# Seven block products in another order across two PSUM banks, with a re-ordered operand split and a new table of rank offsets

## The chip, the cores and the metric

One NeuronCore of one Trainium2 chip. The metric is the device time of one execution in microseconds (us), as a median of several runs. A profile is one further execution of the same program, with its own time.

## The reference

Attention on q, k, v of shape 8 x 8 x 576 x 64 (batch, head, position, channel): a softmax attention over positions averaged in fours, repeated back to 576 positions, plus a softmax attention in a band of 7 positions. The sum is laid out as 4608 rows of 512 and goes through a two-layer block:

```python
    x = np.ascontiguousarray(attn_out.transpose(0, 2, 1, 3)).reshape(B * S, H * D)   # 4608 x 512
    h = x @ w_in                        # 512 x 2048
    g = np.maximum(0.01 * h, h)
    return (g @ w_out).astype(np.float32)   # 2048 x 512
```

Nearly all of TensorE's work is the two matrix products.

## The kernel before

Every fp32 matrix product is made of three fp32r matmuls (high x high, high x low, low x high parts), so each operand exists as a high and a low half. The 4608 rows are cut into twelve chunks of 256 to 512 columns. The first nine chunks use a plain product (line 1120) for the first layer. The last three chunks have 512 columns each, and their first layer is worked out with seven block products in place of eight (a Strassen-Winograd scheme) for each pair of blocks of the 2048 features: eight groups for a chunk, 24 groups in all, which I number G0 to G23. This runs from about 640 us to the end.

A group is the function `products`. It has two PSUM banks. Bank b1 holds the halves y and v, bank b2 the halves z and x; a half is 128 x 256. A block product is six matmuls of 256 columns into one half (line 1149). In the order in which TensorE's queue has them before the change, with the scheme's numbers:

- product 1 into x (b2), product 2 into y (b1), product 5 into v (b1), product 7 into z (b2), product 6 into x (b2, on top of 1), product 3 into v (b1, on top of 5), product 4 into z (b2, on top of 7).

Beside them, with `mix` as one SBUF tile of three thirds: ScalarE (ACT) copies product 1 out of x and later the sum "u2" out of x (both line 1158), and product 5 out of v (1158). VectorE (DVE) makes the joint sum p57 of products 5 and 7 (line 1179: one of them read from its bank, the other from `mix`). At the end DVE adds two thirds of `mix` to each whole bank (line 1164), `leaky` applies the activation with two ACT instructions (1210, 1211) and a DVE subtraction (1213), and the result is gh, gl, of which there are three buffers each.

The second layer (`down_proj`, line 1245) takes gh and gl. Its unit is three matmuls of 512 columns into one of four accumulators; a group yields eight such units, which I call "downs". They have no tie to a place between the products: a planner (class `Order`) puts all work into one order ahead of time, by modelled start times, ranks, and the offsets of the table `SHIFTS` (task number: offset of its rank). The queue of each engine is then fixed, and an instruction on the chip waits by semaphores for what it needs, as tracked for whole tiles.

Weights of products 5, 6, 7 and 3 are sums of blocks that come from DRAM in each group: `feed` loads r0 (blocks of products 5 and 6) and then r1 (blocks of products 7 and 3), 512 KB each, from the POOL queue (line 588). There is one buffer of each, so r0 is asked for after product 6 of the group before, and r1 after its product 3.

`operands` makes the seven right-hand operands T0 to T6 of a chunk (`split`: an ACT copy and a subtraction, lines 471 and 474; `less`: a DVE subtraction into PSUM, line 481). T0 to T6 belong to products 1, 2, 5, 6, 7, 3, 4 in this order.

Of the kernel before, what the change touches and what calls it, by code (L numbers as in the profile page):

```python
# [13 lines left out]
ALU = mybir.AluOpType  # L14
# [29 lines left out]
HN = 256  # L44
# [27 lines left out]
def pieces(j0, j1):  # L72
# [13 lines left out]
RATE = 270e3  # L86
SAFE = 0.4
SHIFTS = {
# [16 lines left out]
}  # L105
POLICIES = [SHIFTS]
SCARCE, HURRY = ("pt",), 1000
# [139 lines left out]
def attn_moe(policy, ctx, tc, qkt, vd, vs3, qkb, vb, vwb, band, identb, w_in, w_out, ident, out, sums):  # L247
    nc = tc.nc
# [8 lines left out]
    od = Order(bufs, policy)  # L257

    def slot(*tags):
        return (yield ("slot", tags, 0))  # L260
# [16 lines left out]
    def op(eng, n, *after, times=1, port=False):  # L277
        if eng == "PE":
            dur = n
        else:  # L280
            a, k = COST[eng]
            dur = times * a + k * n
        return (yield ("op", eng, dur, max((0.0,) + after), 0, port or eng == "POOL"))
# [9 lines left out]
    def wait(name, n=1):  # L293
        return (yield ("wait", name, n))
# [144 lines left out]
    def bank_of(s):  # L439
        return (s // 3 + FIRST + 1) % 2  # L440
# [15 lines left out]
    def operands(i):  # L456
        tx = yield from wait(("x", i), LANDED[i])
        (b11, t1), (b21, b22) = ([x[:, :, :HN], x[:, :, HN:]] for x in xt[i])

        def taken(s):  # L460
            if i == FIRST:
                t = yield from wait(("up", LAST[-1])) if s == 6 else wait(("emptied", bank_of(s)))
            h = yield from slot(f"t{s}")
            if i == FIRST:
                h.t = t
            return h

        def split(s, h, x, t, own=True):
            hi, lo = put(i, s)
            t = yield from op("ACT", 2 * HN, t, h.t)  # L470
            nc.scalar.copy(out=hi, in_=x)
            eng = pick("DVE", "POOL") if own else "DVE"
            t = yield from op(eng, 2 * HN, t, port=own)
            (nc.vector if eng == "DVE" else nc.gpsimd).tensor_tensor(out=lo, in0=x, in1=hi.bitcast(F32), op=ALU.subtract)  # L474
            od.signal(("T", i, s), t)
            ready[i, s] = h
            return t

        def less(out, x, y, *after, port=False):
            t = yield from op("DVE", 2 * HN, *after, port=port)  # L480
            nc.vector.tensor_tensor(out=out, in0=x, in1=y, op=ALU.subtract)
            return t

        h = yield from taken(0)
        yield from split(0, h, b11, tx)
        h = yield from taken(1)
        yield from split(1, h, b21, tx)
        h = yield from taken(2)
        yield from split(2, h, t1, tx)
        s_2, s_3 = yield from two("pt")  # L490
        t2 = bank(s_2).rearrange("p (c m) -> p c m", c=2)
        t = yield from less(t2, b22, t1, tx, s_2.t, port=True)
        t3 = bank(s_3).rearrange("p (c m) -> p c m", c=2)
        tt = yield from less(t3, t2, b11, t, s_3.t)
        h = yield from taken(3)
        t = yield from split(3, h, t2, t, False)
        t = yield from less(t2, b21, t2, t, tt)
        h = yield from taken(4)
        s_3.free((yield from split(4, h, t3, tt, False)))
        h = yield from taken(5)  # L500
        tb = yield from split(5, h, b22, tx)
        h = yield from taken(6)
        t = yield from split(6, h, t2, t, False)
        s_2.free(t)
        return max(t, tb)
# [86 lines left out]
    def pick(*engines):  # L592
        return min(engines, key=lambda e: od.engine[e] + (0.5 if e == "POOL" else 0.0))
# [534 lines left out]
    def products(i, ch, j):  # L1128
# [4 lines left out]
        mix = sb(s_m, [128, 3 * HN], F32)  # L1133
# [3 lines left out]
        def product(out, ws, s, first, *after):  # L1137
            to = yield from wait(("T", ch, s))
            held = None
            if isinstance(ws, int):  # L1140
                after += ((yield from wait(("fed", ch, j, ws // 2))),)
                held = fed.pop((ch, j, ws // 2)) if ws % 2 else None
                x = odd[ws // 2][0]
                ws = tuple([x[:, ws % 2, k, c * 128:c * 128 + 128] for c in range(2)] for k in range(2))
            t = yield from op("PE", 0.702, to, *after)
            (wh, wl), (xh, xl) = ws, put(ch, s)
            for c in range(2):
                for k, (a, b) in enumerate(((wh, xh), (wh, xl), (wl, xh))):
                    nc.tensor.matmul(out, a[c], b[:, c], start=first and c + k == 0, stop=c == 1 and k == 2, skip_group_check=True)  # L1149
            if held:  # L1150
                held.free(t)
            if last:
                ready[ch, s].free(t)
            return t

        def copied(name, out, src, t):
            t = yield from op("ACT", HN, t, s_m.t)
            nc.scalar.copy(out=out, in_=src)  # L1158
            od.signal((name, i), t)
# [7 lines left out]
        a11, a12, a22 = block(2 * j, 0), block(2 * j, 1), block(2 * j + 1, 1)  # L1167
        tw = max((yield from wait(("w", 2 * j, 0))), (yield from wait(("w", 2 * j + 1, 0))))
        t = yield from product(x, a11, 0, True, tw, s_2.t)
        od.spawn(-10, copied("p1", mix[:, :HN], x, t))  # L1170
        yield from product(y, a12, 1, True, s_1.t)
        t = yield from product(v, 0, 2, False)
        od.spawn(-10, copied("p5", mix[:, 2 * HN:], v, t))
        t = yield from product(z, 2, 4, False)

        def joint(t):
            t5 = yield from wait(("p5", i))
            t = yield from op("DVE", HN, t, t5)
            nc.vector.tensor_tensor(out=mix[:, 2 * HN:], in0=z, in1=mix[:, 2 * HN:], op=ALU.add)  # L1179
            od.signal(("p57", i), t)  # L1180

        od.spawn(-10, joint(t))
        tc1 = yield from wait(("p1", i))
        t = yield from product(x, 1, 3, False, tc1)
        od.spawn(-10, copied("u2", mix[:, HN:2 * HN], x, t))
        tc5 = yield from wait(("p5", i))
        t1 = yield from product(v, 3, 5, False, tc5)

        def first(t):
            t = yield from added("b1", b1, 0, t, (yield from wait(("u2", i))))  # L1190
# [1 line left out]
            od.spawn(-10, leaky(i, 2 * HN, s_1, b1, t))  # L1192

        od.spawn(-10, first(t1))
        tm = yield from wait(("p57", i))
        t2 = yield from product(z, a22, 6, False, tm)

        def second(t):
            t = yield from added("b2", b2, 1, t, (yield from wait(("u2", i))))
# [219 lines left out]
```

## Time and profile before

| | |
|---|---|
| median of 3 runs | 928.11 us (927.41 to 929.78) |
| the profiled execution | 926.15 us |
| its span, first to last instruction | 924.4 us |
| TensorE (PE) matmuls busy | 896.7 us, 97% |
| PE weight loads (PEld) busy | 841.2 us, 91% |
| DVE, ACT, POOL busy | 657.8, 459.8, 616.4 us |

PE works on its matmuls in a pipeline, so a gap reads best on PEld, the weight load ahead of each matmul: there is one for each matmul, and its row says how long it sat idle and what ended that.

### The profile page before, as it was taken

What the parts mean: (1) busy time and instruction counts of PE and PEld (TensorE: products, weight loads), DVE (VectorE), ACT (ScalarE), POOL (GpSimd) and SP (SyncE); (2) the same over time, 40 slices, a digit from 0 to 9 for tenths busy, and PEclk for the clock granted to TensorE, in tenths of its full rate; (3) what the DMA queues carried; (4) which work ended last, traced back from release to release, by engine and by line L of the source; (5) the groups of instructions that cost most, each with busy time, mean ns of one, the idle gap of its engine ahead of it and who ended that gap; (6) DMA issues with size and microseconds to landing.
All of it is one profiled execution on the core that took longest, in us unless ns stands there. A gap on an engine that the chain in (4) does not pass through costs nothing.

```text
span 924.4 us, 17453 instructions
## 1 busy us (share of the span) xinstructions
PE 896.7 (97%) x6400; PEld 841.2 (91%) x6400; DVE 657.8 (71%) x1134; ACT 459.8 (50%) x1426; POOL 616.4 (67%) x354
## 2 busy tenths in 40 slices
PE   5899999999999999999999999999999999998998
PEld 4699999999999999999999999999888888887886
DVE  4787778879788988888687778774776786333222
ACT  3678565455355465455456545444563454343322
POOL 4565778889988788876786797973878686021000
PEclk8699999999999999999999999999999999999999
DMA  9769556546546646465444644642766555324321
GB/s 262 247 210 337 173 174 207 187 151 202 162 139 189 199 160 203 147 209 181 146 157 150 188 140 150 211 139 65 252 213 200 157 188 157 109 75 131 116 91 45
DMA packets 65461, 157.64 MB, mean 171 GB/s; under 512 B 7440, under 2 KB 20496, under 8 KB 65376
## 3 DMA queue, kind: packets, MB, share of 16 engines
q1 hardware_dynamic: 58320, 131.23, 44.7%
q0 software_dynamic: 6912, 25.17, 8.6%
q8 instruction: 50, 0.82, 0.4%
q14 instruction: 35, 0.29, 0.1%
q10 hardware_dynamic: 144, 0.13, 0.0%
HBM read 138.16 MB, written 18.35 MB: 169 GB/s over the span
## 4 chain that ended last, share of the span: by engine, by line
PE 85%; DVE 4%; issue 4%; ACT 3%; DMA 2%; POOL 2%; SPq 0%; DVEq 0%; POOLq 0%; ACTq 0%
PE acc L1245 40%; PE hp L1120 27%; PE hp L1149 7%; PE pt L1149 3%; PE pt L1051 1%; PE pt L750 1%; PE pt L772 1%; PE pt L786 1%; DMA r<-sums 1%; POOL prod L947 1%; DVE mix L1179 1%; ACT mix L1158 1%; DMA qk<-in_qkt_dram 1%; DVE s L954 1%; DVE xl L474 1%
## 5 line engine op out<-in xcount | busy, mean ns | idle before, releaser
L1005 POOL TENSOR_TENSOR prod<-v,s 128x1344 f32<-128x1344 f32 (+2 forms) x96 | 263.2, 2746 | 27.7 <-DVE xloc L1012 16.4
L947 POOL TENSOR_TENSOR prod<-k 128x1365 f32<-128x1365 f32 (+2 forms) x96 | 249.3, 2600 | 43.2 <-DVE xloc L1012 17.3
L1245 PE MATMUL acc<-gh,w 128*128 128x384 f32 (+3 forms) x768 | 208.9, 340 | 0.4 <-ACT o L1289 0.4
L1210 ACT ACTIVATE gh<-hp 128x384 fp32r<-128x384 f32 (+3 forms) x176 | 85.1, 483 | 172.6 <-PE acc L1245 141.9
L1120 PE MATMUL hp<-xh,w 128*128 128x384 f32 (+2 forms) x576 | 146.3, 323 | 0.6 <-DVE gl L1213 0.6
L1245 PEld LDWEIGHTS acc<-gh,w 128*128 128x128 f32 x768 | 137.5, 188 | 9.9 <-issue 1.0
L1213 DVE TENSOR_TENSOR gl<-hp,gh 128x384 fp32r<-128x384 f32 (+3 forms) x176 | 95.0, 541 | 62.8 <-ACT hp L1211 61.2
L954 DVE TENSOR_REDUCE s<-prod 128x21 f32<-128x1365 f32 (+2 forms) x96 | 133.0, 1385 | 3.0 <-POOL prod L947 2.6
L1012 DVE TENSOR_REDUCE xloc<-prod 128x192 f32<-128x1344 f32 (+2 forms) x96 | 131.0, 1366 | 4.0 <-POOL prod L1005 2.8
L1245 PE MATMUL acc<-gh,woh 128*128 128x384 f32 (+3 forms) x384 | 132.0, 344 | 0.1
L1245 PE MATMUL acc<-gl,w 128*128 128x384 f32 (+3 forms) x384 | 129.8, 338 | 0.0
L1245 PE MATMUL acc<-gl,woh 128*128 128x384 f32 (+3 forms) x384 | 129.4, 337 | 0.0
L1245 PE MATMUL acc<-gh,wol 128*128 128x384 f32 (+3 forms) x384 | 129.4, 337 | 0.0
L1120 PEld LDWEIGHTS hp<-xh,w 128*128 128x128 f32 x576 | 101.3, 188 | 2.9 <-issue 1.8
L1120 PE MATMUL hp<-xl,w 128*128 128x384 f32 (+2 forms) x288 | 91.6, 318 | 0.0
L588 POOL DMA_DIRECT2D r<-sums x48 | 26.6, 554 | 90.3 <-PE hp L1149 42.8
L1211 ACT ACTIVATE hp<-hp 128x384 f32<-128x384 f32 (+3 forms) x176 | 84.3, 479 | 0.0
L1120 PE MATMUL hp<-xh,w_even 128*128 128x384 f32 (+2 forms) x288 | 76.0, 325 | 1.3 <-DVE gl L1213 1.2
L1245 PEld LDWEIGHTS acc<-gh,wol 128*128 128x128 f32 x384 | 72.1, 188 | 4.3
L1245 PEld LDWEIGHTS acc<-gh,woh 128*128 128x128 f32 x384 | 72.1, 188 | 4.1 <-issue 0.8
L1245 PEld LDWEIGHTS acc<-gl,w 128*128 128x128 f32 x384 | 72.2, 188 | 3.9
L1245 PEld LDWEIGHTS acc<-gl,woh 128*128 128x128 f32 x384 | 72.2, 188 | 3.0 <-DVE gl L1213 0.3
(276 smaller groups left out, 1688.8 us busy)
## 6 DMA issues: line engine op xcount, KB each, us to landing
k<-in_qkb_dram SPq DMA_DIRECT2D x64, 390.0 KB, 4.3
r<-sums POOLq DMA_DIRECT2D x48, 512.0 KB, 4.8
qk<-in_qkt_dram SPq DMA_DIRECT2D x32, 576.0 KB, 6.4
v<-in_vb_dram SPq DMA_DIRECT2D x64, 288.0 KB, 2.9
qk<-in_vs_dram SPq DMA_DIRECT2D x28, 384.0 KB, 3.7
k<-in_qkb_dram SPq DMA_DIRECT2D x28, 325.0 KB, 2.9
v<-in_vb_dram SPq DMA_DIRECT2D x28, 256.0 KB, 2.8
sums<-stage SPq DMA_DIRECT2D x8, 512.0 KB
```

What stands on the lines that cost most here:

```text
L474: (nc.vector if eng == "DVE" else nc.gpsimd).tensor_tensor(out=lo, in0=x, in1=hi.bitcast(F32), op=ALU.subtract)
L588: nc.gpsimd.dma_start(out=odd[n][0].rearrange("p b k m -> p (b k m)"), in_=sums[j, n])
L947: nc.gpsimd.tensor_tensor(out=prv, in0=view(half(s_k), 0, [[DE, nj], [1, DE]]).unsqueeze(2).to_broadcast([128, nj, W, DE]), in1=view(half( ...
L954: nc.vector.tensor_reduce(out=s[:, p, :nj], in_=prv, axis=AX.X, op=ALU.add)
L1005: nc.gpsimd.tensor_tensor(out=prv, in0=view(half(s_v), 0, [[1, nj], [nv, D], [1, W]]), in1=s[:, p, :nj].unsqueeze(2).to_broadcast([128, nj ...
L1012: nc.vector.tensor_reduce(out=xl_t[:, :nj, p], in_=prv, axis=AX.X, op=ALU.add)
L1120: nc.tensor.matmul(hp[:, :n], column_of(wt, c), column(x, c), start=k == 0, stop=k == 3 * NC - 1)
L1149: nc.tensor.matmul(out, a[c], b[:, c], start=first and c + k == 0, stop=c == 1 and k == 2, skip_group_check=True)
L1210: nc.scalar.activation(out=gh[:, :n], in_=hp[:, :n], func=AF.Prelu, alpha=0.01)
L1211: nc.scalar.activation(out=hp[:, :n], in_=hp[:, :n], func=AF.Prelu, alpha=0.01)
L1213: nc.vector.tensor_tensor(out=gl[:, :n], in0=hp[:, :n], in1=gh[:, :n].bitcast(F32), op=ALU.subtract)
L1245: nc.tensor.matmul(acc[:, :n], wt[:, es], g[:, :n], start=f == f0 and j == 0, stop=f == f1 - 1 and a == len(fs) - 1 and j == 2)
```

## The change

The queue order of products 5 and 7 is swapped: 1, 2, 7, 5, 6, 3, 4, which goes b2, b1, b2, b1, b2, b1, b2. ACT copies product 7 (not 5) into the last third of `mix`, and the joint sum reads product 5 from bank b1. The planner's waits move with it: product 6 waits for the copies of 1 and 7, product 3 for the joint sum, product 4 for the copy of u2. The operands are made in the order T0, T1, T4, T2, T3, T5, T6. All numbers of `SHIFTS` are new, for tasks from number 31 on, which is all tasks of the kernel after its first constant loads and tile holders.

```diff
 SHIFTS = {
-    31: 1.6, 32: 6.8, 33: -6.4, 34: 14.7, 36: -51.1, 37: 2.9, 38: -6.5, 39: 12.3, 40: 34.3, 41: 1.7, 42: -0.5, 43: -8.2, 44: 5.6, 45: 2.6,
...
+    31: -0.4, 32: 3.2, 33: -6.4, 34: 13.8, 36: -34.5, 37: 8.1, 38: -6.5, 39: 13.3, 40: 88.1, 41: -0.5, 42: -6.6, 43: -9.8, 44: 3.4, 45: 4.1,
...
         h = yield from taken(1)
         yield from split(1, h, b21, tx)
-        h = yield from taken(2)
-        yield from split(2, h, t1, tx)
         s_2, s_3 = yield from two("pt")
...
         tt = yield from less(t3, t2, b11, t, s_3.t)
+        h = yield from taken(4)
+        s_3.free((yield from split(4, h, t3, tt, False)))
+        h = yield from taken(2)
+        yield from split(2, h, t1, tx)
         h = yield from taken(3)
         t = yield from split(3, h, t2, t, False)
         t = yield from less(t2, b21, t2, t, tt)
-        h = yield from taken(4)
-        s_3.free((yield from split(4, h, t3, tt, False)))
...
         yield from product(y, a12, 1, True, s_1.t)
+        t = yield from product(z, 2, 4, False)
+        od.spawn(-10, copied("p7", mix[:, 2 * HN:], z, t))
         t = yield from product(v, 0, 2, False)
-        od.spawn(-10, copied("p5", mix[:, 2 * HN:], v, t))
-        t = yield from product(z, 2, 4, False)
 
         def joint(t):
-            t5 = yield from wait(("p5", i))
-            t = yield from op("DVE", HN, t, t5)
-            nc.vector.tensor_tensor(out=mix[:, 2 * HN:], in0=z, in1=mix[:, 2 * HN:], op=ALU.add)
+            t7 = yield from wait(("p7", i))
+            t = yield from op("DVE", HN, t, t7)
+            nc.vector.tensor_tensor(out=mix[:, 2 * HN:], in0=v, in1=mix[:, 2 * HN:], op=ALU.add)
             od.signal(("p57", i), t)
 
         od.spawn(-10, joint(t))
         tc1 = yield from wait(("p1", i))
-        t = yield from product(x, 1, 3, False, tc1)
+        tc7 = yield from wait(("p7", i))
+        t = yield from product(x, 1, 3, False, tc1, tc7)
         od.spawn(-10, copied("u2", mix[:, HN:2 * HN], x, t))
-        tc5 = yield from wait(("p5", i))
-        t1 = yield from product(v, 3, 5, False, tc5)
+        tm = yield from wait(("p57", i))
+        t1 = yield from product(v, 3, 5, False, tm)
...
-        tm = yield from wait(("p57", i))
-        t2 = yield from product(z, a22, 6, False, tm)
+        tu = yield from wait(("u2", i))
+        t2 = yield from product(z, a22, 6, False, tu)
```

## Rows read from the trace of the kernel before

**Rows 1.** Windows: us, busy us (instructions) of PE, PEld, DVE, ACT, POOL, clock, DMA

```profile
45.00:640.00 595.00, 592.54 (x4377) 577.99 (x4375) 480.73 (x818) 321.71 (x1042) 468.45 (x225) 1.00 0.55 177
...
730.00:850.00 120.00, 114.39 (x702) 100.61 (x701) 64.24 (x101) 49.53 (x134) 49.04 (x42) 1.00 0.42 131
```

**Rows 2.** Waits, 636 to 925 us: who waits for whom, us, times, longest

```profile
ACT mix L1158 <- DVE mix L1179: 34.0, 22, 5.0
...
PEld hp L1149 <- ACT mix L1158: 5.3, 13, 0.5
...
PEld pt L1149 <- DMA r<-sums: 3.8, 2, 2.8
PEld pt L1149 <- ACT mix L1158: 3.7, 8, 0.5
```

**Rows 3.** Timeline of G19 from product 7, and G20's start: start, us, engine

```profile
858.28 0.19 PEld L1149 LDWEIGHTS pt<-xh,r 128*128 128x128 f32 x1
...
859.83 0.79 PEld L1149 LDWEIGHTS pt<-xl,r 128*128 128x128 f32 x6
...
860.21 0.42 DVE L1179 TENSOR_TENSOR mix<-pt,mix 128x256 f32<-128x256 f32 x1 [4.92 <-PE pt L1149]
...
860.66 0.37 ACT L1158 COPY mix<-pt 128x256 f32<-128x256 f32 x1 [0.87 <-DVE mix L1179]
861.09 0.77 PEld L1149 LDWEIGHTS pt<-w,w_odd 128*128 128x128 f32 x6 [0.47 <-ACT mix L1158]
...
861.23 0.53 POOL L588 DMA_DIRECT2D r<-sums  x1 [0.18 <-issue]
...
863.55 0.37 ACT L1158 COPY mix<-hp 128x256 f32<-128x256 f32 x1 [2.52 <-PE hp L1149]
...
863.91 0.19 PEld L1245 LDWEIGHTS acc<-gh,woh 128*128 128x128 f32 x1
...
865.20 0.89 PEld L1149 LDWEIGHTS hp<-xl,r 128*128 128x128 f32 x6
```

**Rows 4.** Line 588 (loads of r), 860.4 to 861.6 us

```profile
DMA to landing us min/median/max: 3.5/4.2/4.8
```

**Rows 5.** Line 588, 741 to 743 us (the loads for G9)

```profile
DMA to landing us min/median/max: 3.9/5.3/6.7
```

**Rows 6.** Line 588, 830 to 834 us (the loads for G17)

```profile
DMA to landing us min/median/max: 5.5/5.8/6.1
```

**Rows 7.** Timeline at the starts of G9 and G17: PEld, POOL, DVE

```profile
742.41 0.53 POOL L588 DMA_DIRECT2D r<-sums  x1 [0.45 <-PE hp L1149]
...
744.17 0.19 PEld L1149 LDWEIGHTS pt<-xh,w_even 128*128 128x128 f32 x1
...
745.17 0.69 DVE L1213 TENSOR_TENSOR gl<-hp,gh 128x512 fp32r<-128x512 f32 x1 [0.18 <-ACT hp L1211]
...
745.30 0.77 PEld L1149 LDWEIGHTS pt<-xl,r 128*128 128x128 f32 x6 [0.94 <-DMA r<-sums]
...
833.37 0.54 POOL L588 DMA_DIRECT2D r<-sums  x1 [0.15 <-issue]
...
835.06 0.69 DVE L1213 TENSOR_TENSOR gl<-hp,gh 128x512 fp32r<-128x512 f32 x1
...
835.22 0.19 PEld L1149 LDWEIGHTS pt<-xh,w_even 128*128 128x128 f32 x1
...
838.24 0.77 PEld L1149 LDWEIGHTS pt<-xl,r 128*128 128x128 f32 x6 [2.83 <-DMA r<-sums]
```

**Rows 8.** Chain of work that ended last: start, us, what (the downs after G20)

```profile
870.40 6.30 PE acc L1245 x27
```

**Rows 9.** Timeline of ACT at the start of G21

```profile
876.03 0.60 ACT L1210 ACTIVATE gh<-hp 128x512 fp32r<-128x512 f32 x1 [1.72 <-PE acc L1245]
876.52 0.59 ACT L1211 ACTIVATE hp<-hp 128x512 f32<-128x512 f32 x1
877.49 0.37 ACT L1158 COPY mix<-pt 128x256 f32<-128x256 f32 x1 [0.37 <-ACT hp L1211]
```

31 rows, old and new, of the table SHIFTS are left out of this document.

## The prediction

> **What bounds the kernel now.** I read the windows first. From 45 to 640 us PE's matmuls are busy for 592.5 of 595 us at a granted clock of 1.00 [rows 1], the upper of its two levels (2.4 GHz): PE sets the end, and time is won only where it sits idle. From 730 to 850 us it is busy for 114.4 of 120 [rows 1]; the reader should see that the gaps are in the stretch of the block products. The waits name them [rows 2]: the first weight load of a block product waited for ACT's copies into `mix` 13 + 8 = 21 times, 5.3 + 3.7 = 9.0 us, and for a load of r twice, 3.8 us. I count PEld's rows alone, since the matmul rows repeat the same gaps.
>
> The timeline says which product waits [rows 3]. In G19 product 7 starts at 858.28, products 6 and 3 follow without a gap, each 0.7 us, and product 3's loads start at 859.83. The joint sum needs product 7 alone, which was through by about 859.2, but starts at 860.21, after product 6: both write bank b2. ACT's copy of u2 follows at 860.66, right after the joint sum (both write the tile `mix`; 34.0 us of such waits in 22 groups [rows 2]), ends at 861.03, and only then does product 4, which writes b2 as well, start: 861.09, after 0.47 us of idle. So two of the seven neighbours share a bank (5 after 2 in b1, 6 after 7 in b2), and the second pair makes a chain of DVE, ACT and PE with only product 3 to cover it.
>
> The wait is for the bank, not for the address, since z and x don't overlap. The Trainium skill says the same ("PSUM — Partial Sum Buffer", section "PSUM bank collisions raise a hardware error"): two engines in one bank and quadrant collide also in disjoint columns, so PSUM is guarded by bank. By that rule the alternation does not take bank waits away; it gives each of them one product of cover. That is where it could speak against the change: more of the neighbours than before have a bank wait between them. The steps below price this from rows.
>
> **The change part by part.** The sum is made against the profiled execution, 926.15 us (span 924.4 and 1.75 around it); the median of the runs, 928.11, stands 1.96 above it, and I take the difference over.
>
> (a) *The wait ahead of product 4 goes.* After the change the joint sum is no longer ahead of product 6 in bank b2, and u2 is copied while product 3 runs in b1. Gain: 9.0 us [rows 2].
>
> (b) *Each product from the third on now waits for a reader one product back.* G20's start gives the price [rows 3]: product 1's copy starts at 863.55 and ends at 863.92, while product 2's last weight load is followed at 863.91. Product 4 started 0.06 us after its copy's end (861.03 to 861.09). So with nothing in between, product 7 can start at 863.98 in place of 863.91: 0.07 us. The same holds for product 6 behind the copy of 7, and for product 4 behind u2. Product 3 behind the joint sum costs 0.05 more, as that takes 0.42 against 0.37 us: 0.12. A down (0.7 us) in between hides each of these. The new code gives the planner explicit waits at products 6, 3 and 4, so it will put downs there where it has any; at product 7 it has none. In the queue of before I count 14 of 24 groups with nothing, or only a transpose, between products 2 and 5: 14 x 0.07 = 1.0 us. For the other three places (0.26 together) the bounds are 0 and 24 x 0.26 = 6.2; I take four groups, the ones that start a chunk and one more, 1.0 us, nearer the lower end since each group makes eight downs and needs three here.
>
> (c) *Loads of r at the start of a chunk.* Where no downs are left (G9 and G17), PE waited for r0: 0.94 and 2.83 us [rows 7]. Now the third product needs r1, which is asked for second. It landed 6.7 us after 742.41, at 749.1 [rows 5, 7], and 6.1 us after 833.37, at 839.5 [rows 6, 7], 1.3 to 3.8 us after r0. Product 2's last load is at 744.17 and 835.22 [rows 7], and without the waits of (a) some 0.4 earlier, so it is through at 743.9 and 834.9. Without cover that is 5.2 + 4.6 = 9.8 us, 6.0 more than now. But the first downs of the group before are ready with gl, at 745.86 and 835.75 (start and duration of line 1213 [rows 7]), ahead of r1, and four of them take 2.8 us: PE then waits 2.0 + 0.4 and 0.9 + 0.9, 4.2 us. With eight downs it would be 2.9. I take 4.2, a loss of 0.4 against 3.8, since the downs lie before r1's landing in both places.
>
> (d) *The same load in all other groups.* In G19 r1 is asked for at 861.23 and lands at most 4.8 us later, 866.0 [rows 3, 4]; product 5 started at 865.20 [rows 3], on r0, after three downs. Product 7 in this place would wait 0.8 us, and 0.47 more as product 4's wait is gone: 1.27 us. Two more downs (1.4 us) hide it. They exist: after G20 there are 27 matmuls, nine downs in one run [rows 8], which were put off. Eight groups have this tight pattern (three downs or fewer between product 3 and product 5): bounds 0 and 8 x 1.27 = 10.2 us. I take 0, since the planner knows when the loads land and only has to draw on the downs put off.
>
> DMA: no load is added and the queue's order (r0, then r1) stays. The Trainium skill's fit ("DMA: Bandwidth & Descriptors", section "Anatomy of one DMA — SWDGE (gpsimd) path", 2.0 us + bytes / 436 GB/s) gives an estimated 3.2 us for 512 KB. The fastest landing here is 3.5 us [rows 4], but the second of the pair takes 4.8, so the fit would put (d) at nothing where the rows bound it at 1.27 a group.
>
> (e) *Operands.* T2 is now made after the PSUM slots are free, T4 earlier. This moves one ACT copy and one subtraction of 0.7 us each, behind the downs that fill PE between chunks; T2 belongs to the fourth product now, and T4 to the third, so the order matches. Cost 0 while those downs last; 0.7 us for each of three chunks, 2.1, if not.
>
> (f) *The offsets.* They move work in the whole kernel. From 45 to 640 us there is little to win: 2.5 us of idle in all [rows 1]. I take 0, within 4 us either way.
>
> Sum: -9.0 + 1.0 + 1.0 + 0.4 = -6.6 us. 926.15 - 6.6 = 919.55 for a profiled execution, 921.5 for the median.
>
> **The rivals.** *r1 becomes the wait* (c and d without their downs): six or more of the eight tight groups wait, about 7.6 us, and the gain shrinks to nothing: about 929 us. For it: r1 lands last and is now needed first. Against it: eight downs a group, and three or four in use there.
>
> *ACT has other work ahead of product 1's copy.* Product 7 waits for that copy through the bank, but the new code gives the planner no wait there, so it can put the activation's pair just ahead of the copy (lines 1210 and 1211, from 876.03 to 877.11, 1.1 us [rows 9]). At G21 the copy comes 0.37 us after the pair's end [rows 9], so a small shift is enough. One such collision costs up to 1.1 us. The point from which it decides is 6.6 / 1.1, six groups; with ten of the 24 it is 11.0 us, 4.4 slower than before: 932.5. Against it: ACT is busy for only 49.5 of 120 us [rows 1], and the downs of (d) ahead of product 7 hide it.
>
> *The change does not do what it says, or the offsets pay it back:* products stay next to each other in one bank at other places, or new gaps ahead of 640 us take some 7 us: 928. And the other way: the waits for r go as well (3.8) and (b) is covered, 926.15 - 12.8, and 915.3 as a median.
>
> **How the numbers follow.** A measurement of this kernel tells about 0.3% (2.8 us) from no change. My forecast of 921.5 (917.5 to 925.3) has 0.58; everything covered (915 to 917.5) 0.08; r1 as the wait (926 to 930) 0.14; the gain paid back elsewhere (925.5 to 931) 0.10; ACT ahead of the copy (931 to 937) 0.10. Faster by over 0.3%: 0.58 + 0.08 = 0.66. Within 0.3%: 0.14 + 0.07 = 0.21. Slower: 0.10 + 0.03 = 0.13. The range leaves out the slower cases and the very best: 915.8 to 930.5.
>
> **What would show it.** (a) right: no wait of a weight load for line 1158 of 0.4 us and over ahead of product 4, and the sum of these waits under 3 us; the joint sum starts about 0.4 us after product 5's last load, not after product 6. (b) right: gaps of 0.05 to 0.15 us ahead of products 7, 6, 3 and 4. (c) right: waits for r of some 4 us, in two groups; the rival shows six or more of about 1 us. ACT's rival shows waits of 0.5 us and over for line 1158 ahead of product 7 with lines 1210 and 1211 just before the copy. (f) wrong: PE busy for less than 590 of the 595 us. The prediction is wrong if the waits for `mix` stay near 9 us, or if the time goes to stretches ahead of 640 us.

## The result and the profile after

| | before | after |
|---|---|---|
| median of the runs that stood beside each other | 928.94 us (927.41 to 929.78, 4 runs) | 917.62 us (916.3 to 922.04, 4 runs) |
| the same, measured once more on another occasion | 927.74 us (924.82 to 930.64, 7 runs) | 918.05 us (913.95 to 921.23, 4 runs) |
| ratio | | 0.9888 (95% interval 0.9849 to 0.9927), once more 0.9888 (0.9843 to 0.9933) |
| the profiled execution, its span | 926.15, 924.4 us | 918.87, 917.1 us |

The change makes the kernel 1.1% faster, some 10 us. The two profiled executions, both at a mean granted clock of 0.987, are 7.3 us apart. In the new file the lines have moved: block products 1150 (1149 before), copies 1159 (1158), joint sum 1180 (1179), activation 1212, 1213 and 1215 (1210, 1211, 1213), downs 1247 (1245), loads of r 589 (588).

The windows of the changed kernel, as in [rows 1] (us, busy us of PE, PEld, DVE, ACT, POOL, clock, DMA):

```profile
45.00:640.00 595.00, 593.32 (x4382) 578.97 (x4382) 476.12 (x813) 321.95 (x1042) 470.88 (x226) 1.00 0.55 176
...
730.00:850.00 120.00, 117.12 (x734) 104.78 (x732) 65.87 (x102) 51.61 (x138) 50.23 (x43) 0.99 0.45 139
```

PE's idle time from 45 to 640 us is 1.7 us (2.5 before), from 730 to 850 it is 2.9 (5.6 before). The waits of the weight loads, 636 us to the end, as in [rows 2] (who waits for whom, us, times, longest); the list is whole for the block products, their line being 1150:

```profile
PEld hp L1150 <- issue: 3.1, 4, 2.5
PEld hp L1150 <- ACT mix L1159: 2.2, 2, 1.9
PEld acc L1247 <- DVE gl L1215: 0.9, 1, 0.9
PEld pt L1150 <- ACT mix L1159: 0.6, 1, 0.6
PEld hp L1150 <- DVE mix L1180: 0.4, 1, 0.4
...
PEld pt L1150 <- issue: 0.4, 2, 0.2
...
PEld pt L1150 <- DMA r<-sums: 0.3, 1, 0.3
```

The waits for copies into `mix` fell from 9.0 us in 21 to 2.8 in 3, and none of the three stands ahead of product 4. Those of the block products together fell from 13.0 (the rows of [rows 2] and one of 0.2) to 7.0 us. G19 from its product 7, as in [rows 3]:

```profile
852.16 0.19 PEld L1150 LDWEIGHTS hp<-xh,r 128*128 128x128 f32 x1 [0.23 <-issue]
...
852.86 0.79 PEld L1150 LDWEIGHTS hp<-xl,r 128*128 128x128 f32 x6
...
853.18 0.37 ACT L1159 COPY mix<-hp 128x256 f32<-128x256 f32 x1 [2.90 <-PE hp L1150]
853.95 0.43 DVE L1180 TENSOR_TENSOR mix<-hp,mix 128x256 f32<-128x256 f32 x1 [3.25 <-PE hp L1150]
854.16 0.90 PEld L1150 LDWEIGHTS hp<-xh,r 128*128 128x128 f32 x6
...
854.59 0.60 ACT L1212 ACTIVATE gh<-pt 128x512 fp32r<-128x512 f32 x1 [1.04 <-PE acc L1247]
854.99 0.79 PEld L1150 LDWEIGHTS hp<-xl,r 128*128 128x128 f32 x6
...
855.60 0.38 ACT L1159 COPY mix<-hp 128x256 f32<-128x256 f32 x1
...
857.02 0.89 PEld L1150 LDWEIGHTS hp<-w,w_odd 128*128 128x128 f32 x6
```

Product 7 starts at 852.16, product 5 at 852.86. Its neighbour, product 6, starts only at 854.16, after a down. The joint sum starts at 853.95, right behind product 5, and ends at 854.38, before product 3 at 854.99. The copy of u2 comes after an activation pair and is through at 855.98; product 4 follows at 857.02, after two downs. Only product 7 waits, 0.23 us. Such a down stands between products 5 and 6 in 22 of the 24 groups, and one or two between products 3 and 4 in 19; in the queue before, products 7, 6, 3 and 4 ran without any down between them in 22 groups.

### The profile page after: what moved, and what is told of

Read it like the earlier page. It is cut to its first block, busy times and chain, and to the rows that moved or that the text cites. A ratio compares the mean times of both kernels' runs of the same rounds, so it can differ in the third digit from the quotient of the medians.

```text
span 917.1 us, 17462 instructions
## 1 busy us (share of the span) xinstructions
PE 893.2 (97%) x6400; PEld 841.5 (92%) x6400; DVE 656.9 (72%) x1133; ACT 461.1 (50%) x1426; POOL 617.7 (67%) x355
## 4 chain that ended last, share of the span: by engine, by line
PE 90%; DVE 4%; ACT 2%; DMA 1%; POOL 1%; issue 1%; SPq 0%; ACTq 0%; POOLq 0%; DVEq 0%
PE acc L1247 42%; PE hp L1121 28%; PE hp L1150 8%; PE pt L1150 4%; PE pt L1052 1%; PE pt L751 1%; PE pt L787 1%; PE pt L773 1%; DMA qk<-in_qkt_dram 1%; DVE s L955 1%; POOL prod L948 1%; DVE xloc L1013 0%; DMA out_dram<-o 0%; DVE xl L475 0%; ACT pds L692 0%
## 5 line engine op out<-in xcount | busy, mean ns | idle before, releaser
L1247 PE MATMUL acc<-gh,w 128*128 128x384 f32 (+3 forms) x768 | 213.2, 340 | 0.5 <-ACT o L1291 0.5
```

The costliest lines, as they stand in the source:

```text
L1247: nc.tensor.matmul(acc[:, :n], wt[:, es], g[:, :n], start=f == f0 and j == 0, stop=f == f1 - 1 and a == len(fs) - 1 and j == 2)
```

## Experiments

Times are medians; each ratio is to runs of the kernel before beside it.

**The parts alone.** The new order with the old table, and the old order with the new table; in both only the table `SHIFTS` is exchanged against that of the other kernel:

```diff
 SHIFTS = {
-    31: -0.4, 32: 3.2, 33: -6.4, 34: 13.8, 36: -34.5, 37: 8.1, 38: -6.5, 39: 13.3, 40: 88.1, 41: -0.5, 42: -6.6, 43: -9.8, 44: 3.4, 45: 4.1,
+    31: 1.6, 32: 6.8, 33: -6.4, 34: 14.7, 36: -51.1, 37: 2.9, 38: -6.5, 39: 12.3, 40: 34.3, 41: 1.7, 42: -0.5, 43: -8.2, 44: 5.6, 45: 2.6,
...
```

> The new product and operand order with the old table of offsets. Theory A (the order with its waits carries the gain): the waits of the block products' weight loads for copies into mix fall from 9.1 us to under 3, and the time to 917 to 921 us. Theory C (the new offsets carry it): the time stays at 926 to 930 us.

Measured: 923.49 us, ratio 0.9955 (0.9935 to 0.9975). The waits of its weight loads (block products 1149, downs 1246):

```profile
PEld acc L1246 <- DVE gl L1214: 5.8, 6, 2.3
PEld pt L1149 <- issue: 5.7, 6, 1.9
...
PEld hp L1149 <- ACT mix L1158: 0.5, 1, 0.5
```

The waits for `mix` are down to 0.5 us, as theory A said, but only 4 us are won, and the time misses that theory's 917 to 921. In their place stand 5.8 us of downs that wait for gl, and 5.7 us ahead of product 7. These are its loads of r1: one was issued at 834.08 with a landing time of 5.8 us and one at 853.37 with 6.4, that is at 839.9 and 859.8, and the two longest waits end there (PEld of this kernel):

```profile
839.98 0.19 PEld L1149 LDWEIGHTS pt<-xh,r 128*128 128x128 f32 x1 [1.92 <-issue]
...
859.87 0.19 PEld L1149 LDWEIGHTS pt<-xh,r 128*128 128x128 f32 x1 [1.74 <-issue]
```

> The old product and operand order with the new table of offsets. Theory A: the 0.47 us waits ahead of product 4 stay (about 20, some 9 us) and the time is 926 to 931 us. Theory C: 917 to 921 us.

Measured: 935.59 us, ratio 1.0095 (1.0068 to 1.0122), slower than the kernel before by 8 us and outside both forecasts. Its waits for `mix` rise to 14.1 us; 17 of the 19 stand ahead of product 4, as before:

```profile
PEld hp L1150 <- ACT mix L1159: 10.4, 11, 3.9
PEld pt L1150 <- ACT mix L1159: 3.7, 8, 0.5
```

Neither part does it alone: the order gives 4 us of the 10, the table by itself costs 8. The table belongs to its order: the new order loses 5 to 6 us with the old table, the old order 8 with the new one. "Order" here is the products, the planner's waits and the operands together; the order of the operands was not run by itself.

**Bank or tile.** In the kernel before, product 5's copy and the joint sum get a tile of their own, `jt`, and the sum into b2 becomes two halves (the tile used by `summed` is cut the same way). PE's queue is the same, instruction for instruction.

```diff
-        od.spawn(-10, copied("p5", mix[:, 2 * HN:], v, t))
+        od.spawn(-10, copied("p5", jt, v, t))
...
-            nc.vector.tensor_tensor(out=mix[:, 2 * HN:], in0=z, in1=mix[:, 2 * HN:], op=ALU.add)
+            nc.vector.tensor_tensor(out=jt, in0=z, in1=jt, op=ALU.add)
```

> The kernel before with the copy of product 5 and the joint sum in an SBUF tile of their own (so that the copy of u2 and the joint sum no longer write one tile), and for that the last sum into bank b2 in two halves; the order of PE's queue is the same, instruction for instruction. If the copy of u2 waits for the joint sum because of the common tile, as the prediction says, it starts at product 6's end, 0.45 us earlier, the wait ahead of product 4 falls from 0.47 to about 0.1 us, and the time is 919 to 922 us. If it waits because both read bank b2, nothing changes: 0.47 us waits and 926 to 930 us.

Measured: 925.82 us, ratio 0.9982 (0.9960 to 1.0004): no change that can be told. The waits for `mix` are 5.4 and 3.8 us in 13 and 8, as before. Its timeline in one group:

```profile
863.38 0.42 DVE L1188 TENSOR_TENSOR jt<-pt,jt 128x256 f32<-128x256 f32 x1 [4.94 <-PE pt L1154]
...
863.84 0.37 ACT L1163 COPY mix<-pt 128x256 f32<-128x256 f32 x1 [0.89 <-DVE jt L1188]
...
864.26 0.77 PEld L1154 LDWEIGHTS pt<-w,w_odd 128*128 128x128 f32 x6 [0.48 <-ACT mix L1163]
```

The two instructions no longer write one tile, and the copy still waits for the joint sum to end (863.80). What they have in common is bank b2, which both read, and the program tracks it as one tile. So the prediction's reason for this link, the tile `mix`, falls; it is the bank.

**The copy of u2 twice.** One line is added to each kernel, and all queues stay as they were otherwise:

```diff
             nc.scalar.copy(out=out, in_=src)
+            if name == "u2":
+                nc.scalar.copy(out=out, in_=src)
```

> The kernel before with the copy of u2 issued twice in each group (0.37 us more on ACT, same result; all queues otherwise the same, instruction for instruction). If this copy sits on PE's path ahead of product 4, as the prediction says, each of the 21 waits grows by about 0.3 us and the three groups without one get one: 6 to 8 us slower than the kernel before, 934 to 936 us, and the waits for mix rise from 9 to 15 to 17 us. If the copy is off the path, no change.

> The changed kernel with the copy of u2 issued twice in each group, all queues otherwise the same. If product 3 and a down now cover the copy (0.7 + 0.7 us against 0.35 + 0.7 + 0.05), the time does not move: within 1.5 us of the changed kernel, waits for mix within 1 us of its 2.8. If the copy is still on the path, 6 to 8 us slower than the changed kernel.

> The changed kernel once more, for a tighter interval beside the kernel before and for comparison with the experiment on its u2 copy: 916 to 919 us by every theory.

Measured: before with two copies 935.87 us, ratio 1.0076 (1.0048 to 1.0105), 8.1 us slower than before; after with two copies 915.40 us (913.65 to 915.68), the changed kernel beside it 918.05 (913.95 to 921.23). The waits for `mix`, first of before, then of after with the copy doubled:

```profile
PEld hp L1149 <- ACT mix L1160: 10.6, 14, 0.9
PEld pt L1149 <- ACT mix L1160: 7.0, 8, 0.9
```

```profile
PEld hp L1150 <- ACT mix L1159: 2.4, 2, 2.2
...
PEld pt L1150 <- ACT mix L1159: 0.6, 1, 0.6
```

17.6 against 9.0 us before: most of the waits went from 0.47 to 0.9, so the copy was on PE's path there to its full length. In the changed kernel the same 0.37 us cost nothing (3.0 against 2.8). Its median is 2.7 us under that of the changed kernel, more than the 1.5 expected, but that is no gain: its four runs had a mean granted clock of 0.993 to 0.996, and the two runs of the changed kernel at 0.993 and 0.994 took 913.95 and 916.3 us.

**A down in place of the alternation.** In the kernel before the planner is told one more wait, the one that the changed kernel has ahead of product 4:

```diff
         tm = yield from wait(("p57", i))
-        t2 = yield from product(z, a22, 6, False, tm)
+        tu = yield from wait(("u2", i))
+        t2 = yield from product(z, a22, 6, False, tm, tu)
```

> The kernel before in every respect, except that the planner is told that product 4 waits for the copy of u2, as it is told in the changed kernel; it then puts a down (three matmuls, 0.7 us) between products 3 and 4 in 22 of the 24 groups, and the banks do not alternate. Theory A1 (the alternation of the banks is what takes the wait away): products 7 and 6 still share a bank, the joint sum still starts after product 6, and the gain is small, 925 us or more. Theory A2 (a down in that place is enough, whatever the banks): the joint sum and the copy end 0.47 us after product 3, the down takes 0.7 us, so the 21 waits go and the time is 917 to 921 us.

Measured: 926.52 us, ratio 0.9995 (0.9974 to 1.0017): no change. But not for the reason of theory A1 (a down now stands between products 3 and 4 in 21 groups):

```profile
PEld acc L1246 <- DVE gl L1214: 5.5, 3, 4.6
PEld pt L1149 <- DMA r<-sums: 4.8, 2, 3.1
PEld hp L1149 <- ACT mix L1158: 1.1, 4, 0.5
```

The waits for `mix` fell from 9.0 to 1.3 us with products 7 and 6 still side by side in one bank: a down is enough to take them away. The time came back as 5.5 us of waits for gl, 4.6 of it in one place between two chunks, where the downs now ran ahead of what makes their operand, and as 1.0 us more for r. Since a table belongs to its order, this order was given one of its own, by random changes of the offsets that the planner's own order ends earlier with:

> The old order of products with the one added planner's wait ahead of product 4 (a down there), and with a table of offsets searched anew for this order, since a table belongs to its order. Theory A (alternation is needed for the gain): better than the same with the old table (926.5 us), but not under 921 us. Theory B (a down ahead of product 4 and a table that fits are enough): 915 to 920 us.

Measured: 920.35 us, ratio 0.9927 (0.9905 to 0.9948). Its waits in the block products:

```profile
PEld pt L1132 <- DMA r<-sums: 5.4, 2, 3.7
PEld hp L1132 <- ACT mix L1141: 2.5, 6, 0.7
...
PEld pt L1132 <- ACT mix L1141: 0.4, 1, 0.4
```

This lies between the two forecasts, under theory A's 921 and over theory B's 920. Most of the gain needs no alternation: some 7 of 10 us come with one wait told to the planner and a table that fits. The intervals of this kernel (0.9905 to 0.9948) and of the changed one (0.9849 to 0.9927) overlap. Runs at a like mean clock (0.987 and 0.988) say more: 919.89, 920.60 and 921.17 us here against 916.37, 918.26 and 918.87 of the changed kernel, so that one is faster by 2 to 3 us. Whether these belong to the alternation isn't settled by this pair, which differs in the order of the operands and in its table as well.

**The alternation taken back alone.** In the changed kernel products 5 and 7 change places; copies, waits, operand order and table stay:

```diff
-        t = yield from product(z, 2, 4, False)
-        od.spawn(-10, copied("p7", mix[:, 2 * HN:], z, t))
-        t = yield from product(v, 0, 2, False)
+        t5 = yield from product(v, 0, 2, False)
+        t = yield from product(z, 2, 4, False)
+        od.spawn(-10, copied("p7", mix[:, 2 * HN:], z, t))
...
-        od.spawn(-10, joint(t))
+        od.spawn(-10, joint(t5))
```

> The changed kernel with products 5 and 7 swapped back in PE's order (1, 2, 5, 7, 6, 3, 4, so that 7 and 6 are neighbours in bank b2 again); all its other parts stay: the copy of product 7, the planner's three waits, the operand order, the new offsets. The planner then puts two downs between products 7 and 6 where the changed kernel has one, and fewer ahead of product 5. Theory A (alternation saves cover: a wait of one reader needs one down fewer): no wait for mix of 0.4 us comes back, since downs stand there, but the downs are missing elsewhere, as waits for r or gl of 3 to 8 us: 920 to 926 us. Theory B (only the planner's waits and offsets matter, not the banks): 916 to 919 us, as the changed kernel.

Measured: 925.68 us, ratio 0.9991 (0.9970 to 1.0013): the whole gain is gone. In its queue two downs stand between products 7 and 6 (one between 5 and 6 in the changed kernel) and in G10 to G20 one or none (two in G11) ahead of the first product on r, where the changed kernel mostly has three or more.

```profile
PEld pt L1150 <- issue: 4.1, 3, 2.3
PEld hp L1150 <- issue: 3.1, 5, 2.1
PEld acc L1247 <- DVE gl L1215: 3.0, 3, 2.2
PEld pt L1150 <- ACT mix L1159: 2.6, 1, 2.6
PEld pt L1150 <- DMA r<-sums: 2.4, 2, 1.3
```

The waits of the block products rise from 7.0 to 13.6 us (these rows and two of 0.7), some 7.7 of it ahead of products on r and without a 0.47 us wait in each group. This is theory A's picture, the downs are missing elsewhere. The granted clock adds to it: in this profile it is 0.91 from 730 to 750 us and again from 750 to 770, where the kernel before has 1.00 in both. The experiment has the limit of all these pairs, that the table was made for the other order, so that the alternation saves downs is consistent with it but not shown apart from the table.

**The table alone, once more.** The changed kernel with its table searched further:

> The changed kernel with its table searched further from where it stands. All theories: within 2 us of the changed kernel (916 to 920 us), and different waits at the starts of chunks; it shows how much of the time hangs on the table alone.

Measured: 918.20 us, ratio 0.9896 (0.9862 to 0.9930), the same as the changed kernel. Its longest waits are the same ones (2.5 us ahead of product 2 of G9, 1.7 for `mix` in G1). No version run here beats the changed kernel by more than the scatter.

## Why the prediction was right, point by point

**The sum.** 921.5 us was forecast, 6.6 us of gain; measured are 917.62 and 918.05, gains of 11.3 and 9.7 us. The direction, the place and the main term hold; the gain is larger by 3 to 5 us. By the waits of the block products the terms come to -9.0, +3.1, -1.0 and +1.0, together -5.9 us against the -6.6 of the sum. That these lie so close is in part luck: (b) and (d) cost 2.1 us more than forecast, and (c), forecast as a loss of 0.4, was a gain of 1.0.

**(a) The wait ahead of product 4, forecast -9.0: held.** No product 4 waits any more. The doubled copy shows the cause: on the path before, off it after. That the alternation is what took it off is not shown: a down ahead of product 4 did the same in one bank, and the changed kernel has both. One link of the chain had the wrong reason (tile for bank). It changed no number here, but by the wrong reason a tile of its own would have been the cheaper cure, and that bought nothing. The rule that was weighed there, of the Trainium skill's "PSUM — Partial Sum Buffer" ("PSUM bank collisions raise a hardware error"), names reads against reads among the accesses that must be kept apart. In the own-tile run the program does keep them apart (joint sum and copy, both reads of b2, 863.38 to 863.80 and from 863.84).

**(b) One product of cover for each reader, forecast 2.0: 3.1, from fewer and longer waits.** Where nothing stands between products 2 and 7 and no longer wait is named, the starts lie 0.74 to 0.79 us apart in place of 0.70 to 0.72, so 0.07 was of the right size. (In the queue before I count 15 such groups, not 14, which is 0.07 us.) At products 6 and 4 the downs stand as foreseen; product 3 mostly has none of its own, and the down ahead of product 6 covers the joint sum for it. A wait of 0.4 us for the joint sum is left, in G8. What was not in the term is the ACT queue: the 2.8 us for `mix` are three waits behind other work on ACT. The longest, in G1 ahead of product 6 (ACT, then PEld):

```profile
654.38 0.32 ACT L1291 COPY o<-acc 128x192 f32<-128x192 f32 x1 [2.44 <-DMA out_dram<-o]
654.59 0.38 ACT L1159 COPY mix<-hp 128x256 f32<-128x256 f32 x1
```

```profile
655.02 0.77 PEld L1150 LDWEIGHTS hp<-xh,r 128*128 128x128 f32 x6 [1.92 <-ACT mix L1159]
```

The copy of product 7 stood in ACT's queue behind an output copy that waited 2.44 us for its buffer to be stored. That is the rival of the blocked ACT, in three groups and not the six from which it decides, and behind other copies (of an output in G1, of the attention's `outd` in G4, of an operand in G8), not the activation pair. The pair does come ahead of a copy, as in G19 above (854.59 to 855.67), but ahead of u2 with downs behind it.

**(c) Loads of r at the start of a chunk, forecast 4.2 left: mis-sized.** Left are 0.3 us named as r, and 2.5 us ahead of product 2 of G9 from another cause. There the weight load started at 745.84, just after the gl of the group before was made (745.03 to 745.72), which frees the bank that product 2 needs:

```profile
745.03 0.69 DVE L1215 TENSOR_TENSOR gl<-hp,gh 128x512 fp32r<-128x512 f32 x1 [0.98 <-ACT hp L1213]
```

```profile
745.84 0.29 PEld L1150 LDWEIGHTS hp<-xh,w_even 128*128 128x128 f32 x1 [2.47 <-issue]
```

That wait hides the one of the step: r1 of G9 was asked for at 742.24 (line 589) and landed 5.96 us later, at 748.20, so without it product 7, which started at 748.99 after one down, would have waited for r1 instead, by my estimate some 3 us (product 2 through at 744.0, transposes and a down of 1.0 us, then r1). There the step's wait for r1 is covered by another, not gone. In G17 nothing waits: the step supposed that no downs are left at a chunk's start, as in the queue before, where 22 of them ran ahead of G16; in the new one eight run there, and G17 has one after its predecessor and three ahead of product 7, which starts at 832.03, just after r1 landed at 831.92. The step took the planner's stock of downs as given, and the stock was what the change and its table moved.

**(d) r1 in the other groups, forecast 0 with a bound of 10.2: held, with the table.** The changed kernel has three to seven downs ahead of product 7 in G10 to G19 (none in G16) and two in G20, and 1.0 us of waits there in four groups (0.35, 0.24, 0.23, 0.18). The tight pattern stands in seven groups of the queue before, besides G9 and G17, not in eight, so the bound was 8.9. With the old table it is 5.7 us in six groups, so the rival "r1 becomes the wait" was real; it needed exactly the downs that the step spoke of, and the new table is what puts them there.

**(e) Operands, forecast 0: held.** No row of PE waits for an operand's split in the changed kernel; one reaches it through ACT's queue, the 0.6 us in G8 that (b) counts.

**(f) The offsets, forecast 0: the step that missed.** It looked at work ahead of 640 us, where the idle time fell by only 0.8 us. Their worth lies in the block products, as cover: 923.49 with the old table against 918 with the new one, 5 to 6 us. The sum held all the same because (c) and (d) had put the downs in place for nothing, which is what the table does. So this is not what makes the gain larger than the forecast. Of the 10 us the waits of the two profiles account for some 6 (6.0 in the block products, 0.8 from 45 to 640 us, less 0.6 for gl); in the first 45 us PE's idle time is 13.2 us before and 13.4 after. The two profiles themselves are 7.3 us apart, as the profiled execution of the kernel before was a fast one for its clock: 926.15 us at 0.987, where five other runs at 0.987 took 927.2 to 930.2. The rest stays open.

## What to carry to other kernels

A wait of 0.5 us that recurs in every group is closed by work placed in front of it, and that work is a stock: before counting the gain, ask from which place the filler is taken and what it hid there (here loads of r and the making of gl). A hand-made or searched table of offsets belongs to one order of work: the new order lost 5 to 6 us with the old table and the old order 8 us with the new one, so a new order is judged with a table of its own. To see whether an operation is on the path, double it in place with all queues unchanged: 8.1 us against none here.

## What the runs showed of the hardware

The time of one and the same kernel goes with its mean granted clock. Runs of the kernel before took 924.1 us at a mean clock of 0.993, 929.4 at 0.982 and 931.0 at 0.983; the changed one 913.95 at 0.993, 916.4 at 0.988 and 922.0 at 0.981. The windows from 10 to 20, 20 to 30 and 30 to 45 us, first of the profile before, then of the changed kernel with the doubled copy, whose queue on PE is that of the changed kernel (clock is the third number from the end):

```profile
10.00:20.00 10.00, 6.86 (x64) 5.10 (x61) 7.72 (x20) 6.72 (x21) 4.77 (x6) 0.71 1.01 268
20.00:30.00 10.00, 10.00 (x95) 7.51 (x94) 5.32 (x12) 6.65 (x20) 3.93 (x4) 0.50 1.01 337
30.00:45.00 15.00, 11.95 (x125) 9.05 (x122) 11.35 (x27) 10.75 (x33) 9.95 (x10) 0.73 0.59 189
```

```profile
10.00:20.00 10.00, 7.23 (x71) 5.64 (x70) 7.17 (x20) 6.72 (x22) 4.77 (x6) 0.83 1.00 253
20.00:30.00 10.00, 8.51 (x114) 5.90 (x112) 7.92 (x19) 8.25 (x27) 4.85 (x6) 1.00 1.01 333
30.00:45.00 15.00, 11.57 (x148) 9.93 (x148) 11.66 (x27) 12.08 (x36) 11.70 (x11) 0.89 0.71 240
```

Before, PE spent 20 to 30 us wholly at the lower level (0.50, 1.2 GHz); in the other execution that stretch ran at the upper one. In both PE had sat idle ahead of it, for 3.4 and 3.0 us until its weight loads at 15.13 and 15.68 us. The changed kernel itself was seen at 0.90 in one profile and 0.88 in another for that stretch. In the kernel before, the clock is 1.00 from 45 to 910 us, so what its profile lost by the clock it lost almost wholly at the start. It is not so in every profile: in the changed kernel's it is 0.91 from 730 to 750 us, around the wait of 2.47 us in G9, which is 1.8 us of full clock over 20 us (an estimate from the row), while with the doubled copy, after a wait of 2.38 us in the same place, it is 1.00. So a part of the few microseconds between medians of a few runs is luck, and a difference under 3 us between two kernels needs many runs, or runs at a like clock.
